# Dummy matmuls in the buffer of the step that follows, and a new order of steps, in a fused attention and MLP kernel

## The chip, the cores and the metric

One core of one Trainium2 chip. The metric is the device time of one execution in microseconds (us). Before the change it is 350.86 us, the median of 13 runs (348.72 to 353.51).

## What is computed

Attention over 8 batches, 8 heads, 576 positions and head size 64, with 16 extra "beacon" keys ahead of the 576 causal ones, and then a two-layer MLP over the 4608 tokens with an ELU between the layers:

```python
k_all = np.concatenate([beacon_k, k], axis=2)
v_all = np.concatenate([beacon_v, v], axis=2)
scores = scale * np.matmul(q, k_all.transpose(0, 1, 3, 2))
scores = np.where(causal, -1000000000.0, scores)
a = np.exp(scores - scores.max(-1, keepdims=True))
a /= a.sum(-1, keepdims=True) + 1e-09
attn = np.matmul(a, v_all)
...
h = x @ w_in                                  # x: 4608 x 512, w_in: 512 x 2048
g = np.where(h > 0.0, h, np.exp(np.minimum(h, 0.0)) - 1.0)
out = g @ w_out                               # w_out: 2048 x 512
```

## The kernel before, in words

**An order written out.** The kernel defines small steps (functions under `@step`), and a list of 1351 words at its end calls them one by one (L611 on). Each word is a step's name and its numbers, `S.2.6` for example. A manual schedule keeps the list's order on every engine: each engine runs its own instructions in the order of the list, and waits on semaphores where data or a buffer isn't ready. A word such as `ld.3.0.0:V.1.0.1` has a gate: the load is issued only after the step named behind the colon, which sets how early a transfer joins the DMA queues. The list, the gates and the strings of buffer numbers in `slots` come from a planner outside the kernel.

**The steps**, with the engine of each and the lines of before:
- Loads, all issued by GpSimd (POOL), with a cast on the way: `lq` (q and k of batches 0 and 1 to SBUF, L163), `ld` (q and k of later batches, DRAM to DRAM as bf16 in four quarters each, tile `qkd`, L174), `lv` and `lb` (v and beacon v, L191 and L184), `wi` and `wo` (the two weights, L202 and L206).
- q and k have to be transposed. For batches 0 and 1 TensorE does it (`T`, L252, with an identity matrix that step `id` makes), and `cp` copies the result from PSUM on ACT or DVE (its last letter, A or V, L271). From batch 2 on, `ct` issues two DMA transposes on the queue of SyncE (SP), from `qkd` into one of eight `qk` buffers (L266); it needs all eight `ld` of its batch. `cb` adds the beacon keys (L260). A `ct` has the numbers of batch and head pair.
- `S` computes scores of a batch into PSUM (L303), `x` takes their exponential on ACT (L340), `m` applies the causal mask on DVE (L356), `a` adds up partial sums on DVE (L458).
- `L`, `W` (batch 0), `Y`, `Z` (other batches) multiply by ones and by v on TensorE (L369, L474). `n`, `N` take the reciprocal of the sum as Ln and Exp on ACT, `M`, `V` scale the result into the MLP's input `xT` on DVE (L429, L438, L513).
- `F` is the first MLP product (L538), in two halves; `e` (ACT, L551), `r` and `g` (DVE, L556 and L563) are the ELU; `G` is the second product (L579) in eight words per output tile. `o` copies an output tile from PSUM to one of three `osb` buffers (L592), on ACT or DVE by its last letter, and `s` writes it out from SP (L601). The very last tile, `os`, is copied half by DVE and half by ACT into two `osb` buffers and written from two queues (L608, L609).

The MLP of a tile of 512 tokens starts when its batch's attention is done (the first 512 tokens are split in two tiles of 256), so attention of the following batches and the MLP of the earlier ones are interleaved in the list.

**PSUM** is used as four buffers of two banks, tags S0 to S3. Every step that opens a PSUM tile calls `pair`, which takes the next number from the string `slots["S"]`. A buffer is free again when its last reader is done.

**Dummies.** `warm` (L214) issues matmuls on a tile of zeros, in pairs over 64 rows each, to keep TensorE busy where the plan has a gap. Before, each dummy group opens a PSUM tile of its own in the buffer that its word names: `warm.3.512.S.1` is three pairs of 512 columns in S1. There are 16 such words, all in front of the 100th word of the list, with 80 matmuls in all.

Of the kernel before, what the change touches and what calls it, by code (L numbers as in the profile page):

```python
# [17 lines left out]
def kernel(  # L18
# [193 lines left out]

    @step
    def warm(n_, cols, tag, slot_):  # L214

        w = psum.tile([P, 2, 512], FP32, tag=f"{tag}{slot_}", bufs=1, name="w")
        for _ in range(n_):
            for i in range(2):
                nc.tensor.matmul(  # L219
                    out=w[:, i, 0:cols], lhsT=zero[D * i:D * (i + 1), 0:P], rhs=zero[D * i:D * (i + 1), 0:cols],  # L220
                    start=True, stop=True, skip_group_check=True)
# [25 lines left out]
    @step  # L247
    def T(b, p, i):
        dst = tps[b, p, i] = pair("tqk", BF16)[:, 0, :]
        for r in range(R):  # L250
            for h in range(2):
                nc.tensor.transpose(  # L252
                    out=dst[D * h:D * (h + 1), PR * r:PR * (r + 1)],
                    in_=st[b, i][:, 2 * p + h, r, :],
                    identity=identb[0:PR, 0:PR],
                )
# [65 lines left out]
    @step  # L322
    def S_(b, *k_):
        s = sc[(b,) + k_] = pair()
        for (p, c0, c1, o0) in part(b, *k_):
            score(b, p, s, c0, c1, o0)
# [57 lines left out]
    @step  # L384
    def L(b, g):

        if g == "A":
            t = pair("la")[:, 0, :]
            for i in range(2):
                quad(b, i, 0, CUT, t[:, CUT * i:CUT * (i + 1)], None, i == 0)  # L390
            lt[b, g] = t
        else:
            t = pair("lt")
            for i in range(2):
                quad(b, i, CUT, S, t[:, i, 0:S - CUT], None, True)
            lt[b, g] = t[:, :, 0:S - CUT]
# [13 lines left out]
    def W(b, g, *i):  # L410
        half = i[-1]
        k_ = (b, g) + i[:-1]
        if k_ not in ut:
            ut[k_] = pair("ua")
# [67 lines left out]
    def Y(b, g):  # L482

        t = pair("lt")
# [9 lines left out]
    def Z(b, g, half):  # L494
        if (b, g, "t") not in ut:
            ut[b, g, "t"] = pair("ut")
# [26 lines left out]
    def F(t, i, s_):  # L523
# [4 lines left out]
        if s_ == 0:  # L528
            hp[t, i] = pair("hps")
# [38 lines left out]
    def G(t, tp, s_, k_):  # L568
        if s_ == 0 and k_ == 0:
            ob[t, tp] = [pair("ops")]  # L570
# [43 lines left out]
    warm.19.512.S.0 lq.0.1.2.4 lq.0.0.0.2 lq.0.0.2.4 lq.0.1.0.2 lq.0.1.4.8 lq.0.0.4.8 lq.1.0.0.4 id  # L614
    bs lv.0.2 bt T.0.1.0 bk T.0.1.1 cp.0.1.0.A warm.3.512.S.1 cp.0.1.1.V cb.0.0 S.0.1.3 cb.0.1
    cb.0.2 T.0.0.1 x.0.1.3 cb.0.3 S.0.1.1 lq.1.1.0.4:cb.0.2 cb.1.0 cp.0.0.1.V T.0.0.0 x.0.1.1
    S.0.1.2 lb.0:cb.0.0 T.0.2.1 lv.0.1 cp.0.0.0.A cp.0.2.1.V warm.1.512.S.3 warm.1.128.S.3 x.0.1.2
    S.0.0.0 tri warm.2.512.S.2 warm.1.224.S.2 x.0.0.0 T.0.2.0 lv.0.0:cp.0.0.0.A S.0.1.0 cp.0.2.0.V
    T.0.3.0 x.0.1.0 warm.1.512.S.3 warm.1.96.S.3 wi.0.1 cp.0.3.0.V S.0.2.2 T.0.3.1 x.0.2.2
    wi.0.0:cp.0.1.1.V S.0.2.0 cp.0.3.1.V warm.2.512.S.1 warm.1.416.S.1 lv.0.4 x.0.2.0 S.0.3.2  # L620
    S.0.2.3 S.0.3.0 x.0.3.2 m.0.2.0 m.0.0.0 warm.1.512.S.0 warm.1.416.S.0 x.0.3.0 wi.1.0:m.0.2.0
    m.0.1.3 T.1.0.1 cb.1.1 S.0.3.3 x.0.2.3 cp.1.0.1.V lq.1.0.4.8:m.0.1.3 T.1.0.0 x.0.3.3 cp.1.0.0.V
    S.0.0.3 wi.1.1 warm.1.512.S.0 warm.1.384.S.0 m.0.3.2 x.0.0.3 lq.1.1.4.8:cb.0.1 S.1.2 m.0.1.0
    warm.3.512.S.1 warm.1.320.S.1 m.0.3.0 x.1.2.0 wi.2.0 L.0.A wi.3.0:cp.0.2.0.V W.0.A.1 n.0.A
    S.0.0.2 S.0.3.1 W.0.A.0 lv.0.3 x.0.3.1 S.1.0 M.0.A.1 x.0.0.2 wi.2.1 M.0.A.0 T.1.1.1 x.1.0.0
    F.0.0.0 cp.1.1.1.A S.1.1 T.1.1.0 x.1.1.0 F.0.0.1 cp.1.1.0.V wo.2:cp.1.1.1.A m.0.3.3 S.1.5
    m.0.2.2 S.0.0.1 T.1.3.0 x.0.0.1 cp.1.3.0.V e.0.0 S.0.2.1 m.0.0.2 F.0.1.0 m.0.0.3 x.0.2.1 r.0.0
    wo.1:m.0.0.3 F.0.1.1 m.0.2.3 x.1.5.1 wi.3.1:r.0.0 m.0.1.2 g.0.0 T.1.2.1 ld.2.1.144:m.0.1.2 e.0.1
    L.0.B cp.1.2.1.A r.0.1 T.1.2.0 n.0.B cb.1.2 S.1.3 cp.1.2.0.V ld.2.0.288:cb.1.2 g.0.1 T.1.3.1
    x.1.3.1 W.0.B.0.0 x.1.3.0 cb.1.3 cp.1.3.1.V S.1.4 ld.2.0.144:g.0.1 F.0.2.0 x.1.4.1 m.1.0.0  # L630
    W.0.B.0.1 S.1.6 M.0.B.0.0 W.0.B.1.0 x.1.6.2 m.1.3.1 cb.2.0 M.0.B.0.1 W.0.B.1.1 wo.0:M.0.B.0.0
    x.1.6.1 S.1.10 M.0.B.1.1 wo.3:M.0.B.0.1 F.0.2.1 x.1.10.3 M.0.B.1.0 F.1.1.0 ld.2.1.0:M.0.B.1.0
    e.0.2 S.1.9 F.1.1.1 r.0.2 x.1.9.2 m.1.4.1 F.1.0.0 x.1.9.3 g.0.2 ld.2.1.288:r.0.2 e.1.1 S.1.7
    F.1.0.1 m.1.6.1 x.1.7.2 cb.2.1 r.1.1 F.0.3.0 e.1.0 g.1.1 ld.2.0.0:r.1.1 F.1.2.0 r.1.0 S.1.11
    F.0.3.1 cb.2.2 m.1.5.1 x.1.11.3 lb.1:r.1.0 g.1.0 F.1.2.1 ld.2.1.432:m.1.5.1 e.0.3 m.1.10.3
    S.1.12 m.1.1.0 G.0.0.0.0 e.1.2 r.0.3 cb.2.3 G.0.0.0.1 g.0.3 x.1.12.3 lv.1.0:cb.2.3 G.0.0.0.2
    m.1.9.3 cb.3.0 m.1.3.0 m.1.11.3 G.0.0.0.3 ld.2.0.432:m.1.3.0 m.1.2.0 a.1.0.1 F.1.3.0 a.1.1.1
    S.1.8 r.1.2 F.1.3.1 lv.1.1:a.1.1.1 x.1.8.2 a.1.1.2 G.0.0.1.0 g.1.2 e.1.3 lv.1.3:a.1.1.2
    G.0.0.1.1 r.1.3 lv.1.2:g.1.2 G.1.0.0.0 a.1.1.3 g.1.3 lv.1.4:a.1.1.3 G.1.0.0.1 ct.2.0 cb.3.1
    a.1.0.2 G.1.0.0.2 m.1.8.2 m.1.9.2 G.0.0.1.2 a.1.0.3 m.1.12.3 lb.2:m.1.9.2 a.1.1.4 G.0.0.1.3  # L640
    a.1.0.4 lv.2.3:m.1.12.3 m.1.6.2 ct.2.1 o.0.0.V Y.1.0 Z.1.0.0 N.1.0 m.1.7.2 Z.1.0.1 cb.3.2
    a.1.3.1 ct.2.2 S.2.0 a.1.2.1 G.1.0.0.3 lv.2.2:a.1.3.1 x.2.0.0 V.1.0.2 a.1.3.2 S.2.2 a.1.2.2
    G.1.0.1.0 x.2.2.0 V.1.0.0 lv.2.0:a.1.2.2 S.2.1 a.1.3.3 G.1.0.1.1 ct.2.3 x.2.1.0 a.1.3.4 m.2.2.0
    lv.2.1:a.1.3.3 S.2.3 V.1.0.1 G.1.0.1.2 x.2.3.1 lv.2.4:m.2.2.0 S.2.5 x.2.3.0 m.2.3.1
    ld.3.0.0:V.1.0.1 S.2.4 a.1.2.3 x.2.5.1 G.1.0.1.3 m.2.3.0 a.1.2.4 m.2.0.0 ld.3.0.144:m.2.3.0
    S.2.6 x.2.4.1 m.2.5.1 Y.1.1 m.2.1.0 o.1.0.V ld.3.0.288:m.2.5.1 Z.1.1.1 N.1.1 Z.1.1.0 m.2.4.1
    ld.3.0.432:o.1.0.V x.2.6.1 S.2.8 V.1.1.1 x.2.6.2 V.1.1.0 x.2.8.2 S.2.7 a.2.0.1 F.2.0.0
    ld.3.1.0:V.1.1.0 x.2.7.2 m.2.6.1 V.1.1.2 S.2.10 a.2.0.2 F.2.0.1 ld.3.1.144:m.2.6.1 x.2.10.3
    a.2.1.1 a.2.0.3 F.2.2.0 a.2.1.2 e.2.0 m.2.8.2 a.2.1.3 S.2.11 F.2.2.1 x.2.11.3 r.2.0 F.2.3.0
# [124 lines left out]
```

## Time and profile before

| | before |
|---|---|
| median of 13 runs | 350.86 us |
| lowest, highest | 348.72, 353.51 us |
| the profiled execution | 350.86 us |
| its span (first to last instruction) | 349.1 us |
| TensorE (PE) busy | 331.3 us, 95% |
| DVE, ACT, POOL busy | 254.7, 206.8, 99.6 us |
| dummies on PE (L219) in the chain that ended last | 3% |
| end of the last matmul | 343.8 us |

The page of a profile shows, per engine, busy time and its share of the span, then the span in 40 slices with a digit for the busy tenths of each slice, then DMA queues, then the chain of work that ended last, then groups of instructions by source line with their mean length and the idle time ahead of them, and who ended it. PE is the matmul row; PEld is the loading of weights, which overlaps it; a dummy counts as busy. "X <- Y: total, times, longest" in the table of waits says how long X sat idle until Y was done.

### The profile page before, as it was taken

The page shows a single profiled execution, that of the slowest core. Times are in us where ns is not written, and L with a number is a line of the kernel's source. Part 1 is how long each engine was busy: PE and PEld are TensorE (multiplying, and loading weights), DVE is VectorE, ACT ScalarE, POOL GpSimd, SP SyncE. Part 2 cuts the span into 40 slices and gives each one's busy share as a digit, 9 for nine tenths or more (in the row PEclk, how much of TensorE's full clock was granted, in tenths as well). Part 3 has the DMA queues.
Part 4 walks back from the last instruction along what each step waited for, and adds up shares of the span by engine and source line. Part 5 has one row for each costly group of instructions (what it writes and reads, how often), then busy time and mean ns, then how long its engine had stood idle before and what let it go on. Part 6 is the DMA issues. An engine that isn't in the chain of part 4 may idle for free.

```text
span 349.1 us, 10876 instructions
## 1 busy us (share of the span) xinstructions
PE 331.3 (95%) x4716; PEld 186.6 (53%) x4716; DVE 254.7 (73%) x586; ACT 206.8 (59%) x247; POOL 99.6 (29%) x126
## 2 busy tenths in 40 slices
PE   8988999889999899999879999999999999999993
PEld 3556876455555455555435555555455555555551
DVE  1567799789988899799959997598964876685000
ACT  1799872697598795899658668744432343242111
POOL 7664446556181455164333001200000000000000
PEclk9999999999999999999989999999999999999998
DMA  8999999999999999999999834443000000300027
GB/s 130 173 157 201 168 159 103 158 125 89 141 132 201 135 165 94 103 148 92 126 163 98 182 62 30 32 132 124 0 2 2 0 2 0 122 3 0 2 88 274
DMA packets 137536, 35.97 MB, mean 103 GB/s; under 512 B 125712, under 2 KB 132880, under 8 KB 137488
## 3 DMA queue, kind: packets, MB, share of 16 engines
q0 software_dynamic: 102240, 18.49, 70.7%
q1 hardware_dynamic: 34528, 16.39, 23.1%
q8 instruction: 37, 0.61, 0.8%
q10 hardware_dynamic: 720, 0.39, 0.4%
q14 instruction: 11, 0.09, 0.1%
HBM read 37.22 MB, written 16.52 MB: 154 GB/s over the span
## 4 chain that ended last, share of the span: by engine, by line
PE 82%; DMA 6%; DVE 5%; ACT 3%; issue 1%; SPq 1%; DVEq 0%; ACTq 0%
PE hps L538 31%; PE ops L579 31%; PE sc L303 7%; PE ut L369 5%; DMA qk<-qkd 4%; PE w L219 3%; DVE gt L563 2%; ACT et L340 2%; DMA v<-in_v_dram 2%; DVE gt L556 1%; PE lt L369 1%; PE tqk L252 1%; DMA out_dram<-osb 1%; PE ua L369 1%; PE lt L474 1%
## 5 line engine op out<-in xcount | busy, mean ns | idle before, releaser
L538 PE MATMUL hps<-xT,w_in 64*128 64x512 f16 (+1 forms) x1280 | 139.1, 355 | 1.0 <-DVE xT L438 0.3
L579 PE MATMUL ops<-w_out,gt 64*128 64x512 f16 x1152 | 139.2, 378 | 0.0
L340 ACT ACTIVATE et<-sc 128x1024 f16<-128x1024 f32 (+4 forms) x128 | 105.6, 865 | 34.0 <-PE sc L303 32.6
L551 ACT ACTIVATE e<-hps 128x1024 f32<-128x1024 f32 x72 | 72.7, 1023 | 57.2 <-PE hps L538 57.2
L538 PEld LDWEIGHTS <-w_in 64*128 64x128 f16 x1280 | 68.4, 94 | 50.7 <-issue 2.2
L579 PEld LDWEIGHTS <-gt 64*128 64x128 f16 x1152 | 62.4, 94 | 53.6 <-issue 0.9
L563 DVE TENSOR_TENSOR gt<-hps,gt 128x1024 f16<-128x1024 f32 x72 | 87.4, 1221 | 3.2
L556 DVE TENSOR_SCALAR gt<-e 128x1024 f16<-128x1024 f32 x72 | 50.5, 702 | 21.8 <-ACT e L551 21.2
L191 POOL DMA_DIRECT2D v<-in_v_dram x40 | 34.1, 854 | 75.7 <-DVE xT L429 23.8
L356 DVE TENSOR_TENSOR et<-et,triu 128x256 f16<-128x256 f16 (+6 forms) x185 | 38.9, 254 | 10.9 <-ACT et L340 10.9
L303 PE MATMUL sc<-qk 64*128 64x80 bf16 (+20 forms) x528 | 40.2, 250 | 6.9 <-DMA qk<-qkd 4.7
L303 PEld LDWEIGHTS <-qk 64*128 64x128 bf16 x528 | 24.0, 95 | 25.0 <-DMA qk<-qkd 5.5
L458 DVE TENSOR_TENSOR ls<-ls,et 128x672 f16<-128x672 f16 (+2 forms) x84 | 29.0, 367 | 0.3
L174 POOL DMA_DIRECT2D qkd<-in_k_dram x24 | 21.6, 918 | 18.7 <-DVE et L356 5.1
L369 PEld LDWEIGHTS <-v 128*32 128x32 f16 x1248 | 20.7, 96 | 11.2 <-issue 3.4
L174 POOL DMA_DIRECT2D qkd<-in_q_dram x24 | 21.7, 923 | 16.0 <-DVE et L356 7.6
L592 ACT COPY osb<-ops 128x1024 f32<-128x1024 f32 x9 | 9.1, 1009 | 23.6 <-PE ops L579 19.8
L429 DVE TENSOR_TENSOR xT<-ut,rl 128x448 f16<-128x448 f32 (+6 forms) x56 | 20.0, 415 | 0.6 <-ACT rl L504 0.5
L369 PE MATMUL ut<-et,v 128*32 128x512 f16 (+4 forms) x560 | 19.1, 278 | 0.1
L608 DVE COPY osb<-ops 128x512 f32<-128x512 f32 x1 | 0.7, 691 | 24.6 <-PE ops L579 24.6
L503 ACT ACTIVATE rl<-lt 128x576 f32<-128x576 f32 x14 | 9.1, 653 | 14.4 <-PE lt L369 14.4
L458 DVE TENSOR_TENSOR ls<-et 128x928 f16<-128x928 f16 x28 | 17.4, 633 | 0.3 <-PE lt L474 0.2
(45 smaller groups left out, 127.1 us busy)
## 6 DMA issues: line engine op xcount, KB each, us to landing
out_dram<-osb SPq DMA_DIRECT2D x17, 512.0 KB, 4.0
qkd<-in_k_dram POOLq DMA_DIRECT2D x24, 144.0 KB, 4.7
qkd<-in_q_dram POOLq DMA_DIRECT2D x24, 144.0 KB, 4.8
v<-in_v_dram POOLq DMA_DIRECT2D x24, 128.0 KB, 5.5
w_in<-in_moe_w_in_dram POOLq DMA_DIRECT2D x8, 256.0 KB, 7.8
w_out<-in_moe_w_out_dram POOLq DMA_DIRECT2D x4, 512.0 KB, 7.8
v<-in_v_dram POOLq DMA_DIRECT2D x8, 112.0 KB, 4.1
stg<-in_k_dram POOLq DMA_DIRECT2D x3, 288.0 KB, 6.1
```

The costliest lines, as they stand in the source:

```text
L174: nc.gpsimd.dma_start(out=st[b, i][s0:s1], in_=(q, k)[i][b, :, s0:s1].rearrange("h s d -> s h d"))
L191: nc.gpsimd.dma_start(out=v_tile(b)[r0:r0 + n_, j, :, :], in_=v[b, :, ilo[j]:ilo[j] + n_, :].rearrange("h s d -> s h d"))
L303: nc.tensor.matmul(out=s[:, h, o0 + a - c0:o0 + e - c0], lhsT=t[D * h:D * (h + 1), 1, P * j:P * (j + 1)], rhs=t[D * h:D * (h + 1), 0, NB + ...
L340: nc.scalar.activation(out=ets[b, p][:, :, c0:c1], in_=s[:, :, o0:o0 + c1 - c0], func=AFT.Exp, bias=0.0, scale=SCALE)
L356: nc.vector.tensor_tensor(out=o, in0=o, in1=triu[0:kc[j], :, t0:t0 + e - a], op=ALU.mult)
L369: nc.tensor.matmul(out=t[32 * i:32 * (i + 1), a - qa:e - qa], lhsT=ones[0:kc[j], :] if half is None else v16[0:kc[j], j, h, half::2], rhs= ...
L458: nc.vector.tensor_tensor(out=lsum[b, p][0:kc[j], :, qj - q1:], in0=in0, in1=e_[0:kc[j], :, cj:cj + S - qj], op=ALU.add)
L538: both.append(nc.tensor.matmul(out=hp[t, i][:, out_, w * u:w * (u + 1)], lhsT=w_in16[rows, cc, P * fc:P * (fc + 1)], rhs=xt[k_][rows, cc, ...
L551: nc.scalar.activation(out=eb[t, i], in_=hp[t, i], func=AFT.Exp, bias=0.0, scale=1.0)
L556: nc.vector.tensor_scalar(out=rb[t, i], in0=eb[t, i], scalar1=1.0, scalar2=1.0, op0=ALU.min, op1=ALU.subtract)
L563: nc.vector.tensor_tensor(out=gt, in0=hp[t, i], in1=gt, op=ALU.max)
L579: both.append(nc.tensor.matmul(out=o_[out_][:, 0, :] if len(o_) == 2 else o_[0][:, out_, :], lhsT=gts[t, fc][rows, P * (2 * tp + out_):P * ...
```

## The change

The code gets two new helpers and one changed step. `warm` may now name the step that comes next instead of a buffer (`warm.6.496.own.L.0.A`): it opens that step's PSUM tile itself, through `pair`, so in the buffer that the step will use, writes the dummies there and leaves the tile in `made`. The step then takes it through `tile_of`, and overwrites it. For steps `S`, `F` and `G` the dummies are pairs of half rows in both banks, as before; for the others they are single matmuls over all 128 rows in the second bank.

The list of words and the buffer strings are new throughout, from the planner with a second case of late DMA landings beside the first. All steps other than dummies occur as often as before; of the 16 `cp`, four change from DVE to ACT and three from ACT to DVE, and of the output copies `o` one changes to DVE and three to ACT. Dummy words are now 11, with 58 matmuls.

```diff
     slots = {
         "et": (
-            "087625413807256148307521684037512680"),
+            "082476153804276513048725613408752614"),
         "S": (
-            "03210321032013201320123021302013202323201210321301303231010232012121021032031232"
...
+            "03213203120312013012301203210231021212002302130232032120233122302023023123103020"
...
-    @step
-    def warm(n_, cols, tag, slot_):
-
-        w = psum.tile([P, 2, 512], FP32, tag=f"{tag}{slot_}", bufs=1, name="w")
+    def fill(t, n_, cols, halves):
+
         for _ in range(n_):
-            for i in range(2):
+            if halves:
+                for i in range(2):
+                    nc.tensor.matmul(
+                        out=t[:, i, 0:cols], lhsT=zero[D * i:D * (i + 1), 0:P], rhs=zero[D * i:D * (i + 1), 0:cols],
+                        start=True, stop=True, skip_group_check=True)
+            else:
                 nc.tensor.matmul(
-                    out=w[:, i, 0:cols], lhsT=zero[D * i:D * (i + 1), 0:P], rhs=zero[D * i:D * (i + 1), 0:cols],
+                    out=t[:, 1, 0:cols], lhsT=zero[:, 0:P], rhs=zero[:, 0:cols],
                     start=True, stop=True, skip_group_check=True)
+
+    @step
+    def warm(n_, cols, slot_, *word_):
+
+        if slot_ != "own":
+            fill(psum.tile([P, 2, 512], FP32, tag=f"S{slot_}", bufs=1, name="w"), n_, cols, True)
+            return
+        f_, *k_ = word_
+        if f_ == "T":
+            t = pair("tqk", BF16)
+        else:
+            t = pair({"S": "sc", "F": "hps", "G": "ops"}.get(f_, "lt"))
+        made[word_] = t
+        fill(t[:, :, 0:1024].bitcast(FP32) if f_ == "T" else t, n_, cols, f_ in "SFG")
+
+    made = {}
+
+    def tile_of(f_, k_, *how):
+        return made.pop((f_,) + tuple(k_), None) or pair(*how)
...
     def S_(b, *k_):
-        s = sc[(b,) + k_] = pair()
+        s = sc[(b,) + k_] = tile_of("S", (b,) + k_)
...
-            t = pair("la")[:, 0, :]
+            t = tile_of("L", (b, g), "la")[:, 0, :]
...
```

`T`, `W`, `Y`, `Z`, `F` and `G` take their tiles through `tile_of` in the same way. The first words of the two lists:

```diff
-    warm.19.512.S.0 lq.0.1.2.4 lq.0.0.0.2 lq.0.0.2.4 lq.0.1.0.2 lq.0.1.4.8 lq.0.0.4.8 lq.1.0.0.4 id
-    bs lv.0.2 bt T.0.1.0 bk T.0.1.1 cp.0.1.0.A warm.3.512.S.1 cp.0.1.1.V cb.0.0 S.0.1.3 cb.0.1
...
+    warm.13.496.own.T.0.0.0 lq.0.0.0.2 lq.0.1.2.4 lq.0.0.2.4 lq.0.1.0.2 lq.0.1.4.8 lq.0.0.4.8 tri id
+    bs T.0.0.0 lq.1.1.0.4:bs T.0.1.0 T.0.1.1 lq.1.0.0.4 cp.0.1.0.V warm.3.448.own.S.0.1.3 cp.0.1.1.A
+    cp.0.0.0.A S.0.1.3 bt x.0.1.3 S.0.1.2 bk T.0.0.1 x.0.1.2 cb.0.0 warm.2.288.own.S.0.1.0 cb.0.1
+    cp.0.0.1.V S.0.1.0 T.0.2.1 x.0.1.0 m.0.1.2 S.0.1.1 cb.0.2 m.0.1.3 warm.5.432.own.T.0.2.0 cb.0.3
+    x.0.1.1 cp.0.2.1.V T.0.2.0 lq.1.0.4.8:cp.0.2.1.V S.0.0.0 cp.0.2.0.A T.0.3.1
+    warm.1.336.own.S.0.2.3 lv.0.2:cp.0.1.0.V x.0.0.0 cp.0.3.1.V S.0.2.3 S.0.2.2 x.0.2.2 T.0.3.0
+    lb.0:cp.0.3.1.V warm.5.416.own.S.0.3.0 cp.0.3.0.V x.0.2.3 lv.0.0:cb.0.3 S.0.3.0 m.0.2.3 T.1.0.0
+    lv.0.1:bk x.0.3.0 S.0.2.0 cp.1.0.0.V T.1.1.0 x.0.2.0 wi.0.1 S.0.0.2 cp.1.1.0.V T.1.0.1
+    cp.1.0.1.A S.0.3.1 m.0.3.0 warm.2.496.own.S.1.2 wi.0.0:cp.1.1.0.V m.0.0.0 x.0.0.2 S.1.2
+    warm.6.496.own.L.0.A m.0.2.0 wi.1.1 x.1.2.0 m.0.0.2 cb.1.0 wi.1.0:cp.0.3.0.V m.0.1.0 cb.1.1
+    x.0.3.1 lq.1.1.4.8 L.0.A W.0.A.0 n.0.A lv.0.4:m.0.0.0 S.0.3.3 W.0.A.1 wi.2.0:cb.0.2 x.0.3.3
+    S.0.3.2 M.0.A.1 S.0.0.3 lv.0.3:m.0.2.0 x.0.3.2 M.0.A.0 T.1.1.1 wi.2.1:m.0.3.0 x.0.0.3 F.0.0.0
...
```

On SP's queue the order of transposes and output writes, per batch, goes from `s.2.0 s.1.0 ct.4.0 ct.4.1 ct.4.2 s.2.1 ct.4.3` to `s.0.0 ct.4.0 ct.4.1 ct.4.2 ct.4.3 s.1.0 s.2.0`, from `ct.6.0 ct.6.1 ct.6.2 s.3.1 ct.6.3` to `ct.6.0 ct.6.2 ct.6.1 ct.6.3 s.2.1 s.3.1`, and from `ct.3.3 ct.3.0 ct.3.1 ct.3.2` to `ct.3.0 ct.3.1 ct.3.2 ct.3.3`. The last words are these:

```diff
-    G.9.1.0.1 G.9.0.1.2 G.8.0.1.0 G.8.0.1.1 G.9.1.0.2 G.9.0.1.3 G.9.1.0.3 o.9.0.A G.8.0.1.2 s.9.0
-    s.6.1 G.8.0.1.3 s.7.1 G.9.1.1.0 G.9.1.1.1 o.8.0.A G.9.1.1.2 G.9.1.1.3 s.8.0 os.9.1
+    G.8.1.0.3 G.9.1.0.2 G.9.1.0.3 G.8.1.1.0 G.8.1.1.1 G.8.1.1.2 G.9.0.1.1 G.9.1.1.0 G.8.1.1.3
+    G.9.0.1.2 o.8.1.A G.9.1.1.1 G.9.0.1.3 G.9.1.1.2 o.9.0.A G.9.1.1.3 s.9.0 os.9.1 s.8.1
```

## The prediction

> **What bounds the kernel now.** I read the page's slices first, then the stages, then TensorE's waits, then the timeline at each long wait and at the end. In the slices each digit is a tenth of 8.7 us.
>
> ```profile
> PE   8988999889999899999879999999999999999993
> ...
> DVE  1567799789988899799959997598964876685000
> ...
> PEclk9999999999999999999989999999999999999998
> DMA  8999999999999999999999834443000000300027
> ```
>
> TensorE is full from about 185 us to 344 us, so a change can only win in the first 185 us, or after 344 us. The stages (stage, length, then busy time of PE, PEld, DVE, ACT, POOL, granted clock, DMA share, GB/s) say where PE isn't full:
>
> ```profile
> 8.00:26.00 18.00, 15.98 (x328) 9.76 (x330) 10.63 (x32) 14.63 (x20) 11.60 (x17) 1.00 1.39 166
> ...
> 165.00:185.00 20.00, 16.88 (x241) 8.87 (x238) 15.66 (x40) 13.55 (x17) 7.38 (x9) 0.91 1.72 137
> ...
> 205.00:344.00 139.00, 138.82 (x1569) 74.30 (x1565) 87.10 (x138) 56.07 (x62) 4.22 (x5) 1.00 0.17 43
> ```
>
> Busy PE is not useful PE, since the dummies count. So I made a ledger: every PE step of the list at its own pitch in the trace (an F or G step 0.863 us, T 0.376, S 0.2 to 0.3, Y 0.56, Z 0.59). F and G give 248.3 us, all the rest 59.8: 308.1 us of useful work, and the same in both kernels, because the same steps are only reordered. PE ends at 343.8. The lost 35.7 us are 1.3 before its first instruction, 13.6 in dummies (from a dummy's start to the next step's; the first group alone is 6.2) and 20.7 in waits and pitch above these values. The longest waits are for DMAs:
>
> ```profile
> PE sc L303 <- DMA qk<-qkd: 4.7, 2, 3.1
> ...
> PE lt L369 <- DMA v<-in_v_dram: 1.6, 2, 1.3
> ```
>
> The timeline (start, length, what, idle time before it) puts them at three places, a v load at 62 us and transposed q and k at 121 us and 176 us:
>
> ```profile
> 62.63 0.24 PE L369 MATMUL lt<-et,v 128*32 128x64 f16 x8 [1.32 <-DMA v<-in_v_dram]
> ```
>
> ```profile
> 121.57 0.28 PE L303 MATMUL sc<-qk 64*128 64x256 bf16 x2 [1.63 <-DMA qk<-qkd]
> ```
>
> ```profile
> 176.51 0.39 PE L303 MATMUL sc<-qk 64*128 64x256 bf16 x2 [3.05 <-DMA qk<-qkd]
> 176.70 1.91 PE L579 MATMUL ops<-w_out,gt 64*128 64x512 f16 x8
> ```
>
> Against the ledger they cost 1.92, 2.04 and 4.50 us. The third is more than its wait: the eight matmuls after it occupy PE for 1.71 us until the next step instead of 0.86, with the slices' 8 in PEclk at that place.
>
> **What the Trainium skill says.** "TensorE: Matmul & The Clock Gate", part 1 on the HAM clock gate: an idle window of about 3.4 us drops PE to half clock. The trace agrees (3.05 us idle, then a doubled pitch). The same page, part 2, step by step: matmuls stay in program order, so one late operand holds all behind it; at 176 us ready G steps stood behind S.6.6. "DMA: Bandwidth & Descriptors", "Issuing engines are not separate DMA queues": SP's and POOL's transfers interleave on the same 16 engines. The trace agrees: four v loads landed 2.7, 2.5 and 0.5 us apart (57.3, 60.1, 62.6, 63.1) while transposes ran, and 1.0 to 1.2 us apart for larger qkd loads when none did (99.9 to 104.0).
>
> **The change part by part.** Sums are against the profiled execution: 350.86 us, span 349.1, and the median of the 13 runs is 350.86 too.
>
> *Dummies, first matmuls.* The first group goes from 38 half-row matmuls in pairs (6.17 us) to 13 full ones. Nine pairs at 0.43 us ran before the clock rose at 5.07; 13 at that pitch end before 6.9. T.0.0.0 then needs the identity: POOL has issued six loads by 5.37, then tri (0.82) and id (0.70), so 6.9. Before, bt began at 7.58 and S.0.1.3 at 9.51; now T.0.0.0 at 7.0, three T steps, a copy on ACT (0.64) from 8.2: S.0.1.3 at 8.95. From there I followed the longest of PE, ACT and DVE: S.1.2 at 18.5 (was 21.05), the masks of all four pairs done at 20.6, so L.0.A at 20.65 (was 22.41). From L.0.A to F.0.0.0 the trace has 3.49 us (Ln and Exp 1.26, two scalings 1.3): F.0.0.0 at 24.1 instead of 25.90, with 0.16 us more useful work done. Gain: about **2.0 us**. A dummy now takes the buffer of its own step, so it can't start until that buffer is free; the six in front of L.0.A (1.24 us) get theirs at about 18.5 and end by 20, hidden by DVE's masks. If that cover is gone, they cost their full length; all dummies after the first group are 4.96 us, the upper bound. At best this part gains 4.
>
> *Loads of the start.* Three loads for batch 1 (1.6 us of service each) go ahead of v and w_in, and lq.1.0.4.8 waits for cp.0.2.1.V (about 13.0), with lv.0.2 to wi.0.0 queued behind it on POOL. Summing the landing pitches (288 KB 1.6, w_in 1.25, w_out 2.55, qkd 0.95, v 0.55 to 0.65): wi.0.0 lands at about 23 (was 20.1), just in time for F.0.0.0; the last load of batch 2 at 52 to 53 (was 55.8), as more is issued early and the queue stays full. The transposes of ct.2.0 land 7.1 us later (56.0 to 63.1 before): 59 to 60. lv.1.4 has now 2.6 us of PE work between it and the load before it, and lands about 58 to 59.5. PE reaches Y.1.0 at 58.8 (41.5 useful plus 17.3 lost) and S.2.0 at about 60. So most of the 1.92 us goes: **1.3 us**, between 0 and 1.9.
>
> *Transposes, batches 3 to 6.* I count useful PE work between the SP step and its first reader. ct.3.0 to S.3.0: 4.0 before, 6.2 after. ct.4.2 to S.4.6: 5.8, now 6.4. ct.6.2 to S.6.6: 4.8, now 11.0. The trace's need, issue to landing of both halves, is 4.0 to 4.5 us with nothing beside it (ct.6.1, ct.5.1), 6.8 for ct.4.2, 8.4 for ct.6.2. In both slow cases other transfers ran: lv.4.1 to lv.4.3 and the output write s.2.1, lv.6.2 to lv.6.4 and s.3.1. After the change lv.4.0 to lv.4.3 stand ahead of ct.4.0, and no output write stands inside a batch's four transposes: s.0.0 follows ct.3.3, s.1.0 and s.2.0 follow ct.4.3, s.2.1 and s.3.1 follow ct.6.3. Gain at 121 us **1.7** of 2.04 (0 to 2.04), at 176 us **4.4** of 4.5 (2.5 to 4.5), with the half clock, which needs the idle. New risk: ct.3.0 has v loads just before it; I take **0.4** lost, 0 to 1.5. Next late would be DVE: from 74 to 173 us it is busy 89.95 of 99 us, where PE has 92.4 of useful work; the cover for the 1.7 is thin.
>
> *End.* The last output tile uses two of three osb buffers. The lines from before:
>
> ```profile
> 337.86 1.01 ACT L592 COPY osb<-ops 128x1024 f32<-128x1024 f32 x1 [6.80 <-PE ops L579]
> ...
> 343.90 0.69 DVE L608 COPY osb<-ops 128x512 f32<-128x512 f32 x1 [24.59 <-PE ops L579]
> ...
> 345.15 0.59 ACT L608 COPY osb<-ops 128x512 f32<-128x512 f32 x1 [1.49 <-DMA out_dram<-osb]
> 345.76 0.38 ACTq L609 DMA_DIRECT2D out_dram<-osb  x1
> ```
>
> The ACT half waited for s.7.1's landing at 345.07; its own write landed at 347.83, 4.0 us after PE's end, and the span closed 1.3 later. After, s.8.1 is the last word, so 8.1's buffer is still held, and the ACT half must take 9.0's. With PE's end as zero: o.9.0 starts at -1.7 (two G steps remain), s.9.0 issues at -0.6 and lands at about +2.2 (2.8 us, as s.8.0 and s.8.1), copy 0.59, issue, landing 2.07 later: +5.0. s.8.1, behind the DVE half on SP, issues at +1.2 and lands at +4.0 to +4.9. So the end is **1.0 us later** (0.5 to 1.8).
>
> *Copies* that change between ACT and DVE: one more on ACT (0.64), one output copy fewer on DVE: nothing, covered by idle ACT (34 us before et alone).
>
> Sum: 350.86 - 2.0 - 1.3 - 1.7 - 4.4 + 0.4 + 1.0 = **342.9 us**.
>
> **Rivals.** *The stalls move.* All 13 runs lie between 348.7 and 353.5; none shows the 8 us that three absent stalls would give, so the lateness belongs to the list. A new list may bring its own late landings, or DVE, full to 93% from 74 to 173 us once 1.7 us are gone, may hold PE. Then only the start and half of 176 us remain: 350.86 - 2.0 - 2.2 + 1.0 = 347.7. For it: 1.2 us lost in small pieces between 131 and 166 us with no named stall. Against: the longer leads above.
>
> *Slower: the load chain behind lq.1.0.4.8.* POOL issues in order, so if cp.0.2.1.V or what feeds it is late, v, w_in, w_out and batch 2 are late by as much. With the three batch-1 loads not hidden (4.8 us) and the queue empty before lq.1.0.4.8 (the eighth load would land at 14.5, the ninth at 17.5, 1.6 of that service: 1.4) the last load of batch 2 lands at 55.8 + 6.2 = 62.0, ct.2.0 at 69.1, S.2.0 then instead of at 64.6 with 0.6 less work done: 5.1 lost, half clock for one window 1.7 more, and the gains of the first 65 us (3.3) gone: 342.9 + 3.3 + 5.1 + 1.7 = 353.0. It decides once that load lands after about 60. For it: lead ct.2.0 to S.2.0 falls from 4.3 to 3.7. Against: the chain summed above has 6 us of slack to that point.
>
> *No effect:* the waits vary by themselves and the leads are eaten by later issues: 350.9.
>
> **How the numbers follow.** Forecast 0.55 (339 to 346), stalls move 0.24, slower 0.12, no effect 0.09. The range 339 to 350 leaves out the slower case, half of no effect and a few in a hundred below. About 0.5% (1.75 us) can be told from no change: faster 0.76 (forecast, nearly all of the moved stalls), same 0.12, slower 0.12.
>
> **What would show it.** F.0.0.0 near 24 us and S.2.0 near 60; no PE wait for qk above 0.5 us at batches 4 and 6; PEclk without the 8 in mid-span; from PE's last matmul to the span's end 6.3 us instead of 5.3. Wrong would be: a PE wait on v or qk over 2 us anywhere, dummies standing behind a buffer's release, or DVE without gaps where PE idles.

## The result, and the profile after

The changed kernel takes 343.96 us, the median of 11 runs (343.27 to 345.60), against 350.19 us for 48 runs of the kernel before (347.68 to 353.51): a ratio of 0.983, with a 95% interval of 0.981 to 0.986. This ratio, and those of the experiments, leave out the runs that took over 1.5% more than the fastest of their kernel, so they aren't quite the quotients of the medians. The change is worth 6.2 us; the forecast was 342.9. The profiled execution of the changed kernel has a span of 342.7 us, against 349.1.

The slices of the changed kernel's page:

```profile
PE   7979999989999999999999999999999999999992
...
DVE  1667599799999999788999987798876456783000
...
PEclk9999999999999999999999999999999999999999
DMA  8999999999999999999899554421000013003104
```

PE is now nearly full from about 25 us on, apart from an 8 around 72 us; the lower digits that it had around 60, 120 and 175 us and the 8 in PEclk in mid-span are gone. The stages (same columns as in the prediction) say the same in numbers:

```profile
8.00:26.00 18.00, 15.72 (x333) 10.05 (x335) 11.45 (x37) 15.30 (x21) 10.84 (x16) 1.00 1.22 146
...
165.00:185.00 20.00, 19.92 (x361) 11.80 (x358) 19.21 (x51) 15.77 (x20) 9.60 (x11) 1.00 1.36 139
```

From 165 to 185 us PE is busy 19.92 of 20 us at full clock, where it was 16.88 at 0.91. The first stage is no fuller than before (15.72 us against 15.98). In the table of PE's waits no line for `qk` is left, and none for `v`; what leads it now lies in the first 75 us:

```profile
PE hps L560 <- DMA w_in<-in_moe_w_in_dram: 1.4, 1, 1.4
...
PE hps L560 <- DVE xT L451: 1.2, 1, 1.2
...
PE tqk L274 <- DMA stg<-in_q_dram: 0.8, 1, 0.8
```

The timeline of the changed kernel shows those places, then batch 6, then the end:

```profile
25.47 1.05 PE L560 MATMUL hps<-xT,w_in 64*128 64x256 f16 x16 [1.38 <-DMA w_in<-in_moe_w_in_dram]
...
72.07 1.04 PE L560 MATMUL hps<-xT,w_in 64*128 64x512 f16 x8 [1.24 <-DVE xT L451]
...
171.13 0.40 PE L325 MATMUL sc<-qk 64*128 64x176 bf16 x6
171.35 1.04 PE L560 MATMUL hps<-xT,w_in 64*128 64x512 f16 x8
...
336.58 0.69 DVE L630 COPY osb<-ops 128x512 f32<-128x512 f32 x1 [24.62 <-PE ops L601]
...
338.69 0.59 ACT L630 COPY osb<-ops 128x512 f32<-128x512 f32 x1 [2.89 <-DMA out_dram<-osb]
```

F.0.0.0 (first line) waits for w_in. S.6.6 at 171.13 has no idle time in brackets, and the eight matmuls behind it take their normal length. At the end the ACT half waits 2.89 us for the landing of s.9.0, and the span closes 6.2 us after PE's last matmul (336.48), against 5.3 before.

With the ledger of the prediction (lag is the start of a PE step less the useful work done before it), stretch by stretch, the profiled executions against each other:

| Stretch | lag gained before, us | lag gained after, us | gain | forecast |
|---|---|---|---|---|
| to F.0.0.0 | 16.29 | 15.70 | 0.6 | 2.0 |
| F.0.0.0 to S.2.0 (62 us) | 5.08 | 3.48 | 1.6 | 1.3 |
| S.2.0 to Y.3.0 | 3.52 | 4.39 | -0.9 | -0.4 |
| Y.3.0 to F.3.5.0 (batch 4) | 2.27 | 0.23 | 2.0 | 1.7 |
| F.3.5.0 to F.4.6.0 | 1.55 | 1.86 | -0.3 | 0 |
| F.4.6.0 to Y.5.1 (batch 6) | 5.22 | 0.85 | 4.4 | 4.4 |
| PE's end to the span's end | 5.28 | 6.22 | -0.9 | -1.0 |

The seven gains add up to 6.5 us, the span is 6.4 us shorter, and the 0.1 us between them lies in the last 150 us.

### The profile page after: what moved, and what is told of

Its sections match the earlier page's. It is cut to its first block, busy times and chain, and to the rows that moved or that the text cites. A ratio compares the mean times of both kernels' runs of the same rounds, so it can differ in the third digit from the quotient of the medians.

```text
span 342.7 us, 10834 instructions
## 1 busy us (share of the span) xinstructions
PE 329.1 (96%) x4694; PEld 187.0 (55%) x4694; DVE 252.1 (74%) x583; ACT 209.1 (61%) x250; POOL 98.5 (29%) x126
## 4 chain that ended last, share of the span: by engine, by line
PE 85%; DVE 6%; DMA 4%; ACT 2%; issue 1%; POOL 0%; DVEq 0%; ACTq 0%; POOLq 0%
PE ops L601 36%; PE hps L560 32%; PE sc L325 6%; PE ut L391 4%; DVE gt L585 3%; DMA w_in<-in_moe_w_in_dram 2%; PE lt L391 2%; DMA stg<-in_q_dram 2%; PE lt L496 1%; DVE gt L578 1%; PE tqk L274 1%; DVE qk L293 1%; DMA out_dram<-osb 1%; PE ua L391 1%; ACT e L573 1%
## 5 line engine op out<-in xcount | busy, mean ns | idle before, releaser
L362 ACT ACTIVATE et<-sc 128x1024 f16<-128x1024 f32 (+4 forms) x128 | 104.5, 866 | 21.2 <-PE sc L325 19.7
L378 DVE TENSOR_TENSOR et<-et,triu 128x256 f16<-128x256 f16 (+6 forms) x185 | 38.0, 253 | 8.4 <-ACT et L362 8.4
L325 PE MATMUL sc<-qk 64*128 64x64 bf16 (+16 forms) x528 | 39.1, 247 | 0.2
L325 PEld LDWEIGHTS <-qk 64*128 64x128 bf16 x528 | 23.1, 94 | 16.5 <-ACT qk L293 1.4
L614 ACT COPY osb<-ops 128x1024 f32<-128x1024 f32 x11 | 11.1, 1011 | 25.1 <-PE ops L601 25.1
L480 DVE TENSOR_TENSOR ls<-et 128x928 f16<-128x928 f16 x28 | 17.5, 634 | 0.3
```

Of the source, the lines that this page charges most:

```text
L325: nc.tensor.matmul(out=s[:, h, o0 + a - c0:o0 + e - c0], lhsT=t[D * h:D * (h + 1), 1, P * j:P * (j + 1)], rhs=t[D * h:D * (h + 1), 0, NB + ...
L362: nc.scalar.activation(out=ets[b, p][:, :, c0:c1], in_=s[:, :, o0:o0 + c1 - c0], func=AFT.Exp, bias=0.0, scale=SCALE)
L378: nc.vector.tensor_tensor(out=o, in0=o, in1=triu[0:kc[j], :, t0:t0 + e - a], op=ALU.mult)
L480: nc.vector.tensor_tensor(out=lsum[b, p][0:kc[j], :, qj - q1:], in0=in0, in1=e_[0:kc[j], :, cj:cj + S - qj], op=ALU.add)
```

## The experiments

My theory: the transposes of batches 4 and 6 were late because they were issued too few PE steps ahead of their readers and other transfers ran beside them, and the new order mends both; where the dummies write matters little; the tail is dearer. Rivals: the dummies' own tiles give the gain; or output writes inside the transposes alone made the stalls; or the stalls come from the leads alone. Twelve experiments in three groups (1 to 4, 5 to 8, 9 to 12), each beside runs of the kernel before, whose medians in the groups were 349.52, 350.18 and 349.94 us. Ratios are to the runs of the same group.

**1. The dummies taken out.** The list without its ten later dummy words:

```diff
- ... cp.0.1.0.V warm.3.448.own.S.0.1.3 cp.0.1.1.A ...
+ ... cp.0.1.0.V cp.0.1.1.A ...
- ... m.0.3.0 warm.2.496.own.S.1.2 ... S.1.2 warm.6.496.own.L.0.A ...
+ ... m.0.3.0 ... S.1.2 ...
```

> The changed kernel (343.96 us) without its ten later groups of dummies, 4.96 us of PE in all; the first group stays. Dummies are no part of the computation. Theory (they stand where PE would wait anyway): within 0.5%, 342.5 to 345.5, and PE's waits grow by about what the dummies took. Rival (a dummy now waits for its step's own buffer, so it runs late and stands on the path): down to 339, up to 4.96 us faster. Second rival (they keep the clock up): 345.5 to 349, with an 8 or less in PEclk in the first 60 us.

Measured: 346.5 us (342.22 to 347.92), ratio 0.987 [0.981, 0.994]. The time alone can't be told from that of the changed kernel (0.983 [0.981, 0.986]), but the sign that the second rival named is there. The page of this kernel has a 6 in PEclk in the first 60 us:

```profile
PEclk9969999899999999999999999999999999999998
```

The windows (stage, length, PE, PEld, DVE, ACT, POOL, clock, DMA, GB/s) of the changed kernel from 8 to 17.5 us:

```profile
8.00:17.50 9.50, 8.94 (x179) 5.80 (x181) 5.80 (x16) 7.82 (x11) 3.92 (x6) 1.00 1.06 148
```

and of this one from 8 to 24.3 us:

```profile
8.00:17.50 9.50, 6.96 (x160) 4.89 (x156) 7.09 (x19) 9.04 (x13) 4.76 (x7) 1.00 1.24 158
17.60:24.30 6.70, 5.97 (x113) 3.86 (x115) 3.28 (x16) 6.19 (x9) 6.25 (x9) 0.50 1.41 169
```

Without the dummies PE is busy for 6.96 us of the first stretch instead of 8.94, and then the clock stands at 0.50 from 17.5 to 24.4 us. That isn't one trace alone: the mean granted clock of the six runs of this kernel is 0.967 to 0.985, that of 18 runs of the changed kernel 0.991 to 0.999 (and of the six of kernel 3, in the same group as this one, 0.993 to 0.999). So the dummies hold the clock up.

F.0.0.0 came earlier all the same, at lag 13.94 instead of 15.70 (14.82 in another trace of the changed kernel, experiment 5), so dummies stand on the path there as well. At S.2.0 all of it was gone (lag 19.24 against 19.18), because ct.2.0 landed at 61.82, no earlier than elsewhere in the changed list (59.46 in experiment 5). The timeline of this kernel there, and its window:

```profile
61.86 0.60 PE L325 MATMUL sc<-qk 64*128 64x512 bf16 x2 [2.17 <-DMA qk<-qkd]
62.26 1.91 PE L601 MATMUL ops<-w_out,gt 64*128 64x512 f16 x8
```

```profile
62.00:63.00 1.00, 1.00 (x6) 0.30 (x4) 0.00 (x0) 0.50 (x1) 0.14 (x1) 0.50 1.60 164
```

The time saved early became a wait of 2.17 us, and behind it the clock was at 0.50 again: eight G matmuls take 1.91 us. At F.2.0.0 this kernel lags by 22.66, the changed kernel by 21.22.

**2. The dummies' part of the change alone.** The kernel before, order and slots unchanged, with the new `fill`, `tile_of` and `warm`:

```diff
- ... cp.0.1.0.A warm.3.512.S.1 cp.0.1.1.V ...
+ ... cp.0.1.0.A warm.3.512.own.S.0.1.3 cp.0.1.1.V ...
```

> The kernel before, its order and slots unchanged, but every group of dummies after the first writes into the tile of the step that follows it. It is the first half of the change alone. Theory (the gain is in the order, not in where the dummies write): 349 to 352, no difference. Rival (the dummies' own tiles give the gain): 344 to 347. Second rival (they wait for the step's buffer and then delay the step itself): 352 to 355.

Measured: 349.9 us (22 runs), ratio 1.001 [0.999, 1.004]. No difference, as the theory has it, but not because nothing happens. In the trace of the kernel before, the line of the dummies after the first group is this:

```profile
L219 PE MATMUL w<-zero x42: 199/373/387, 8.5 to 22.2; 64*128 64x512 bf16 x28, 64*128 64x416 bf16 x4, 64*128 64x128 bf16 x2, 64*128 64x224 bf16 x2
its engine sat idle before it (us, times) until:
  issue: 2.5, 7
```

PE sat idle 2.5 us ahead of those dummies, and the profile names nobody for it. With the step's own tile the idle time is gone: from the first dummy of each of the eight groups to the step behind them it was 7.32 us in all, and is 4.83 here. (Three of the eight, ahead of `T` and `L` steps, are now also single matmuls over all rows; the five with the same matmuls as before went from 4.36 to 2.81 us.) S.1.2 comes at 19.11 instead of 21.05. But the timeline of this kernel at batch 4 shows where that went:

```profile
113.21 0.39 PE L327 MATMUL sc<-qk 64*128 64x64 bf16 x4 [1.20 <-DMA qk<-qkd]
...
118.94 0.34 PE L327 MATMUL sc<-qk 64*128 64x384 bf16 x2 [2.48 <-DMA qk<-qkd]
...
122.70 0.28 PE L327 MATMUL sc<-qk 64*128 64x256 bf16 x2 [1.58 <-DMA qk<-qkd]
```

The last load of batch 4 was issued 2.7 us earlier than before (100.67 against 103.40) and landed at the same time (110.27 against 110.34). PE came sooner and waited longer: 6.1 us of lag between Y.3.0 and F.3.5.0 instead of 2.27.

**3. The tail undone.** The changed kernel, one word moved:

```diff
- G.9.0.1.2 o.8.1.A G.9.1.1.1 ... s.9.0 os.9.1 s.8.1
+ G.9.0.1.2 o.8.1.A s.8.1 G.9.1.1.1 ... s.9.0 os.9.1
```

> The changed kernel with the output write s.8.1 moved from the last place of the list to directly behind its copy o.8.1.A, so the third osb buffer is free before the end. Theory (the tail grew by 0.94 us because the last ACT copy waits for s.9.0's landing): 342.6 to 343.2, 0.8 to 1.4 us faster, and from PE's end to the span's end 5.0 to 5.4 us instead of 6.2. Rival (the tail is set by the last landing on SP's queue in any case): 343.7 to 344.3, no difference.

Measured: 343.65 us (342.15 to 345.94), ratio 0.983 [0.979, 0.988]. The trace is clear, the time isn't. The timeline of this kernel at its end:

```profile
335.67 0.69 DVE L630 COPY osb<-ops 128x512 f32<-128x512 f32 x1 [24.62 <-PE ops L601]
336.37 0.59 ACT L630 COPY osb<-ops 128x512 f32<-128x512 f32 x1 [1.49 <-DMA out_dram<-osb]
```

The ACT half starts 0.8 us after PE's end (335.56) instead of 2.2, and the span ends 4.8 us after it.

**4. Only the output writes moved, in the old order.** The kernel before, with two words moved:

```diff
- ... s.2.1 cb.4.3 x.4.3.1 a.3.2.2 ct.4.3 ...      ... s.3.1 r.4.7 Z.5.0.0 ct.6.3 ...
+ ... cb.4.3 x.4.3.1 a.3.2.2 ct.4.3 s.2.1 ...      ... r.4.7 Z.5.0.0 ct.6.3 s.3.1 ...
```

> The kernel before with only two output writes moved out of the transposes: s.2.1 behind ct.4.3 and s.3.1 behind ct.6.3. Theory of the writes (a write beside the transposes makes them land late): the waits for qk at 121 and 176 us shrink from 1.63 and 3.05 us to under 0.5, and the time is 344 to 346. Theory of the leads (the transposes were issued too few PE steps ahead of their reader, and the v loads beside them are enough to make them late): both waits stay above 1 us, and the time is 349 to 351.

Measured: 349.64 us (22 runs), ratio 1.000 [0.997, 1.002]. Moving the writes alone gives nothing. Its table of PE's waits has nearly the same sum as before:

```profile
PE sc L303 <- DMA qk<-qkd: 4.6, 3, 3.0
```

In this trace the wait at batch 4 is 3.0 us, though no write is near ct.4.2 (issued at 116.25, landed at 124.41), and the one at batch 6 is 1.02 us: the lag over batch 4 grew from 2.3 to 4.4 us and that over batch 6 shrank from 5.2 to 1.9. Kernel 2, with the write inside, has 6.1 and 2.0 there, so traces of the old list divide the loss between the two places differently, and an effect of the write can't be seen in it.

**5. The changed kernel once more**, without an edit.

> The changed kernel once more, without an edit, beside the runs of this group, since single traces differ by 1 to 2 us in the first 20 us. Expected: 343 to 345 us, 6.2 us from PE's end to the span's end, no wait for qk above 0.5 us at batches 4 and 6, and F.0.0.0 between 24.5 and 26.

Measured: 344.39 us (343.71 to 346.56), ratio 0.987 [0.982, 0.991]; no wait for `qk` at all, the tail again 6.2 us, F.0.0.0 at 24.59 and lag 14.82. So in the start two traces of one kernel differ by 0.9 us, and the gain there is 0.6 to 1.5 us against the trace of before.

**6. Batch 6 of the changed kernel with the old load and the writes inside.**

```diff
- ... m.5.5.1 ld.6.1.432:m.5.3.1 cb.7.0 ...   ct.6.0 ... ct.6.2 ... ct.6.1 ... ct.6.3 ... s.2.1 ... s.3.1
+ ... V.4.1.0 ld.6.1.432:V.4.1.0 ...          ct.6.0 ct.6.1 ... ct.6.2 s.2.1 s.3.1 ... ct.6.3
```

> The changed kernel with batch 6 put back to what it was: its last load (ld.6.1.432) waits for V.4.1.0 again, the transposes stand in the order 0, 1, 2, 3, and the output writes s.2.1 and s.3.1 stand behind ct.6.2, inside them. Theory (the load's lead and the writes made the stall at 176 us): the wait for qk at S.6.6 comes back at 1 to 3 us, with half clock behind it, and the time is 345.5 to 348.5. Rival (the gain at batch 6 comes from elsewhere in the new list): within 0.5% of the changed kernel, 342.3 to 345.5.

Measured: 345.15 us (343.78 to 347.55), ratio 0.988 [0.983, 0.993]. The stall did not come back, so the first theory fails here: ct.6.2, issued at 164.03, landed at 169.80, and PE reached S.6.6 at 170.64. One v load, lv.6.2, was issued beside it at 166.15.

**7. The changed kernel with only the writes inside.**

```diff
- ... e.4.3 ct.6.2 F.4.5.0 ... N.5.0 s.2.1 Z.5.0.1 s.3.1 G.4.0.0.0 ...
+ ... e.4.3 ct.6.2 s.2.1 s.3.1 F.4.5.0 ... N.5.0 Z.5.0.1 G.4.0.0.0 ...
```

> The changed kernel with only the output writes s.2.1 and s.3.1 moved back among batch 6's transposes, behind ct.6.2. Theory of the leads (with the load 19 us ahead of its reader a write inside does no harm): no wait at S.6.6 over 0.5 us, 343 to 345.5, no difference from the changed kernel. Theory of the writes (a write beside the transposes is what makes them late): a wait of 1 us or more at S.6.6 or its neighbours, 345 to 348.

Measured: 344.25 us (343.17 to 345.13), ratio 0.985 [0.980, 0.989]. No difference and no wait for `qk`. (In this trace the clock is at 0.50 from 24.65 to 28.07 us, though its list is the changed kernel's up to the transposes of batch 6: the start varies from trace to trace.)

**8. Two w_in loads early.**

```diff
- ... lq.1.0.0.4 cp.0.1.0.V ... wi.0.1 ... wi.0.0:cp.1.1.0.V ...
+ ... lq.1.0.0.4 wi.0.1 wi.0.0 cp.0.1.0.V ...
```

> The changed kernel with two w_in loads, wi.0.1 and wi.0.0, moved directly behind lq.1.0.0.4, ahead of the waiting lq.1.0.4.8, so that the queue has work from 15 to 17.8 us. Theory (F.0.0.0 waits 1.38 us for wi.0.0, which stands behind that wait, and the gap of 1.4 us in the queue shifts all later loads): no wait for w_in, F.0.0.0 at 24.1 to 24.6, last load of batch 2 about 54, S.2.0 0.5 to 1.3 us earlier, 342.6 to 343.4. Rival (xT on DVE is ready no sooner, so another wait takes its place): F.0.0.0 at 25 or later, no difference. Slower rival (v and the loads of batch 1 land 2.5 us later and hold L.0.A or T.1.3.0): 344.5 to 346.5.

Measured: 344.49 us (343.84 to 345.22), ratio 0.986 [0.982, 0.990]. The rival holds: F.0.0.0 at 25.20. Its table of PE's waits shows three others in place of the one taken away:

```profile
PE ua L391 <- DMA v<-in_v_dram: 0.7, 1, 0.7
PE ua L391 <- ACT rl L426: 0.7, 1, 0.7
PE hps L560 <- DMA stg<-in_k_dram: 0.7, 1, 0.7
```

What went ahead in the queue pushed v and batch 1's k back, as the slower rival said, though not so far that the time shows it.

**9. Batch 6 all back.** As kernel 6, and the v loads earlier as well:

```diff
- ... lv.6.2:g.4.5 ... lv.6.3:V.5.0.0 ... lv.6.4:V.5.0.1 ...
+ ... r.4.3 lv.6.2:r.4.3 ... r.4.4 lv.6.3:r.4.4 g.4.4 lv.6.4:g.4.4 ...
```

> The changed kernel with batch 6 put back as in the run before it (last load late, transposes in the order 0, 1, 2, 3, two output writes inside) and now also the v loads lv.6.2 to lv.6.4 issued among the transposes, as the kernel before had them. Theory of the v loads (they share the engines with ct.6.2, which then takes 7 to 8.4 us instead of 5.8): ct.6.2 lands at 171 to 172.5, S.6.6 waits 0.5 to 2 us for qk, 345 to 347. Rival (the stall needs the whole old list): no wait over 0.3 us, 344 to 345.5.

Measured: 344.24 us (343.61 to 346.07), ratio 0.983 [0.979, 0.988]. The rival holds: no wait. It is close, though: ct.6.2 took 6.7 us (164.07 to 170.77), and PE came to S.6.6 at 170.73. It isn't quite the old case: the v loads were issued at 160.7, 163.0 and 164.3, two of them ahead of ct.6.2, and in the kernel before at 168.0 to 171.1, together with it.

**10. Only the v loads moved, in the old order.** The kernel before, seven words moved:

```diff
- lv.4.1:cb.4.2 ... lv.4.2:V.3.0.1 ... lv.4.3:a.3.3.1 ... ct.4.3 lv.4.4:cb.4.3 ...
+ ct.4.3 ... r.3.2 lv.4.1:V.3.0.0 lv.4.2:V.3.0.0 lv.4.3:V.3.0.0 lv.4.4:V.3.0.0 ...
- ct.6.2 lv.6.2:m.5.7.2 ... lv.6.3:r.4.6 ... ct.6.3 lv.6.4:g.4.6 ...
+ ct.6.2 ... ct.6.3 ... V.5.0.0 lv.6.2:V.5.0.0 lv.6.3:V.5.0.0 lv.6.4:V.5.0.0 ...
```

> The kernel before with only seven v loads moved: lv.4.1 to lv.4.4 wait for V.3.0.0 and lv.6.2 to lv.6.4 for V.5.0.0, so that none is issued among the transposes of batches 4 and 6. Theory of the v loads: ct.4.2 and ct.6.2 land within 5.5 us of their issue instead of 6.8 and 8.4, the waits at 121 and 176 us shrink below 1 us, 345 to 347.5. Theory of the leads (the transposes come too few PE steps ahead of their readers, whatever runs beside them): the waits stay above 1.5 us, 349 to 351.

Measured: 345.32 us (344.74 to 346.87), ratio 0.986 [0.981, 0.991]. Seven loads moved in the old list give 4.6 of the 6 us (3.1 to 6.6 by the interval). Its table of PE's waits:

```profile
PE sc L303 <- DMA qk<-qkd: 1.5, 1, 1.5
PE lt L369 <- DMA v<-in_v_dram: 1.4, 2, 1.1
```

The wait at 176 us is gone (lag from F.4.6.0 to Y.5.1: 0.90 instead of 5.22). The one at batch 4 has only moved from ct.4.2's reader to ct.4.1's: 1.99 us of lag from S.4.0 to F.3.5.0 as against 2.07. So the expectation held in the time and at batch 6; at batch 4 ct.4.2 took 5.9 us, and a wait of 1.5 us stayed. The table of DMA issues shows what changed at batch 6 (transfer, issuing queue, count, KB each, median us from issue to landing), over the issues of ct.6.2 and ct.6.3. First the kernel before, 168 to 174 us:

```profile
v<-in_v_dram POOLq DMA_DIRECT2D x2, 128.0 KB, 6.7
...
qk<-qkd SPq DMA_TRANSPOSE x4, 7.6
```

and the kernel of this experiment, 166.4 to 173.2 us:

```profile
out_dram<-osb SPq DMA_DIRECT2D x1, 512.0 KB, 5.1
qkd<-in_q_dram POOLq DMA_DIRECT2D x1, 144.0 KB, 4.4
qk<-qkd SPq DMA_TRANSPOSE x4, 5.0
```

The four transposes land in 5.0 us instead of 7.6, with the output write and a load still beside them.

**11. Both, in the old order**: kernel 10 with the two writes moved as in kernel 4.

> The kernel before with both edits: the seven v loads as in the run beside it, and the output writes s.2.1 and s.3.1 behind the transposes. Nothing else then runs beside ct.4.2 and ct.6.2. Theory (other transfers, not the lead alone, make them late): 344 to 346.5, waits for qk at batches 4 and 6 below 0.5 us each. Theory of the leads: 348.5 to 351.

Measured: 346.37 us (345.48 to 348.24), ratio 0.989 [0.985, 0.994]. No better than the v loads alone, and at batch 4 1.7 us of lag remain (Y.3.0 to F.3.5.0). Its waits for `qk` are four, two at batch 3 (0.42 and 0.61 us) and two at batch 4 (0.76 and 0.22):

```profile
PE sc L303 <- DMA qk<-qkd: 2.0, 4, 0.8
```

**12. The tail undone, again**: the kernel of 3, for a second time.

> The changed kernel with s.8.1 directly behind o.8.1.A once more, for a second time and trace. Theory (six traces of the changed list and its variants end 6.2 to 6.3 us after PE, the one with this edit 4.8): a tail of 4.7 to 5.0 us again, and 342.5 to 343.5. Rival (the first trace was chance): a tail of 6.2, 344 to 344.5.

Measured: 342.76 us (342.32 to 346.11), ratio 0.980 [0.975, 0.986], with a tail of 5.2 us. The two groups give 0.983 and 0.980, where the changed kernel has 0.983 and 0.987: about 1 us in favour, inside the intervals. The tail of 4.8 and 5.2 us against 6.2 is shown by the traces; that this version is the fastest is likely, and not shown by the times.

## Why the prediction was right, step by step

*The sum.* The forecast was 8.0 us of gain, and 6.2 were measured. That 342.9 lies only 1.1 us from 343.96 is in part luck: the base of the sum, 350.86 from 13 runs, was 0.7 us above the 350.19 of 48.

*Batch 6 (4.4 forecast, 4.4 in the trace)* is right in size. Here too there is luck, since forecast and measurement go by the same trace of the old list. In the traces of kernels 2 and 4 batch 6 costs only 2.0 and 1.9 us, and batch 4 6.1 and 4.4. The two places together are a firmer figure: 7.5, 8.1 and 6.2 us in the three traces of the old order with its v loads in place, 1.1 in the changed kernel, so 5.1 to 7.0 gained where 6.1 was forecast.

In its reasons the prediction named two kinds of transfers beside the transposes, and only one can be seen to count. Set side by side, what ct.6.2 took from issue to its second landing, and how much time PE left it until S.6.6:

| kernel | v loads issued with ct.6.2 or up to 4 us later | write inside | took | time left |
|---|---|---|---|---|
| before | 3 | yes | 8.4 | 5.1 |
| 2: before, dummies' tiles | 3 | yes | 7.1 | 5.8 |
| 4: before, writes moved | 3 | no | about 7.2 | 5.9 |
| 10: before, v loads moved | 0 | yes | at most 6.2 | 6.2 |
| changed | 1 | no | 5.0 | 13.1 |
| 7: changed, writes inside | 1 | yes | 4.5 | 12.6 |
| 6: changed, late load, writes inside | 1 | yes | 5.8 | 6.6 |
| 9: the same, v loads ahead | 1, and 2 just ahead | yes | 6.7 | 6.7 |

(The value of kernel 4 is from the end of PE's wait, since one landing is missing in its trace; that of 10 is a bound, since nobody waited.) Three v loads go with 2 to 3 us more landing time than one or none; a write, issued 2.6 us or more after the first of the pair, with none that can be told. ct.5.1 shows the same the other way round: the changed order puts two v loads beside it, and it took 6.7 to 8.3 us in the nine traces of that order, 4.5 to 6.1 in the five of the old order with none beside it. The v loads are not all, though. In kernels 10 and 11 ct.4.1 took 7.5 and 6.6 us with no v load issued beside it.

The changed kernel mends batch 6 twice: transposes that take 3 us less, and 8 us more time for them. Either is enough, so taking the time back (kernels 6 and 9) brings no stall, and the old list with the v loads alone moved shows that they were the cause there: 0.9 us is lost at batch 6 in the traces of kernels 10 and 11, 1.9 to 5.2 in the three with the v loads in place. (Four loads of batch 4 were moved together with the three of batch 6, so the 4.6 us of kernel 10 belong to both places.)

*Batch 4 (1.7 forecast, 2.0)* has no shown cause. Against the trace of before, kernels 10 and 11 keep 1.7 to 2.1 us of 2.3; against those of kernels 2 and 4, with 6.1 and 4.4 us lost there, the v loads count at this place too (ct.4.2 took 6.8, 8.2 and 8.2 us with them, 5.9 and 5.1 without). For what remains the new order has two things that kernels 10 and 11 haven't. Its last load is earlier: ld.4.1.432 was issued at 100.75 and landed at 107.28, against 103.40 and 110.34, and ct.4.1 waits behind it on SP. And the output writes s.2.0 and s.1.0, which the old order issues together with that load (at 103.41 and 103.93), stand behind ct.4.3. An early issue alone doesn't do it: kernel 2 issued the load at 100.67, with both writes beside it, and it landed at 110.27. No run moved this load or these two writes alone, so longer lead and absent writes are both argued, not shown.

*Loads of the start, at 62 us (1.3, measured 1.6).* Right: no wait for v or `qk` is left there (S.2.0 at 61.80, and 60.65 in the second trace, where 60 was forecast). The last load of batch 2 landed at 55.45 instead of 52 to 53, which left the slower rival 4.5 us short of its point.

*ct.3.0's new risk (0.4 lost, measured 0.9).* Right in sign, wrong in place: nobody waits for ct.3.0. F.2.0.0 waits 1.24 us for `xT`, that is for DVE, which was named as what would be late next.

*The start (2.0 forecast, 0.6 and 1.5 in two traces)* is the term that was mis-sized. Up to L.0.A the marks held within 0.8 us (S.0.1.3 at 9.69 and 8.97 for 8.95; S.1.2 at 19.24 and 18.51 for 18.5; L.0.A at 20.94 and 20.21 for 20.65). The failed step is "from L.0.A to F.0.0.0 the trace has 3.49 us", with wi.0.0 landing at about 23 "just in time": it landed at 25.42 and 24.33, and F.0.0.0 came 4.53 and 4.38 us after L.0.A. Kernel 8 shows that it wasn't this load's place alone: with the load early, F.0.0.0 still stood at 25.20, behind other waits, two of them for transfers. What bounds this stretch as a whole stays open.

*Dummies.* That the tile of the step costs nothing was too simple. It saves 2.5 us of idle PE in the old order (kernel 2), and some of the later dummies stand on the path (kernel 1: 0.9 to 1.8 us by F.0.0.0). Neither gain reaches the end: a wait for `qk` further on takes it back, and in kernel 1 the half clock as well. That the dummies keep the clock up, which kernel 1 shows, stands nowhere in the working.

*End (1.0 later, measured 0.9)*: right, by the wait that was named, and kernels 3 and 12 take it away.

*Copies.* The working counts one output copy fewer on DVE; it is two (three go to ACT, one comes to DVE). No wait of PE in the changed kernel is for such a copy, so the term stays nothing.

*Rivals.* "The stalls move" was refuted in its main point: there is no wait for `qk` in any of the eight traces of the changed list with its dummies. What it was right about is the direction between the terms: in the old order, time gained in the first 60 us (kernel 2) did turn into longer stalls at 120 us. The sum was additive only because the same change took those stalls away.

*The clock.* The Trainium skill, "TensorE: Matmul & The Clock Gate", part 1, says that activity is watched in a free-running window of about 3.4 us. The traces agree, on the halving and on the window: in the clock records of all 14 the stretches between two changes of the clock are whole multiples of 3.41 us (3.41 and 6.83 at half clock; 10.24, 37.55 or 170.67 at full clock). So no length of idle time is a threshold by itself; what seems to count is how much of it falls into one such stretch. In the stretch ahead of the drop at 176 us PE was busy for 0.32 of the time, in that ahead of the drop at 62 us of kernel 1, with its wait of 2.17 us, for 0.36. The wait of 2.48 us in kernel 2 lay across the border of two stretches, the emptier one with PE busy for 0.51, and the clock stayed. That isn't the whole rule either: in kernel 1 the clock fell at 17.5 us after a stretch with 0.72, in kernel 7 at 24.65 us after one with 0.54, both where PE ran short matmuls and transposes.

## What to carry to other kernels

Before a late transfer is issued earlier, look at what is issued in the same microseconds: moving other loads, whose readers come over 20 us later, out of its way gave 4.6 us here with seven words. Compare, for each transfer that an engine waits for, the time from issue to landing with the time that its reader leaves it, and write both down; at batch 6 a remedy on either side was enough. Gains ahead of a place that DMA sets don't count until that place is mended. Take more than one trace before a loss is put down to one place: here three traces of one order divided the same loss in three ways.

## What was unexpected of the hardware

- A dummy group in a PSUM tile of its own costs PE more than its matmuls: 7.32 us for eight groups, against 4.83 us in the tile of the step that follows, with 2.5 us of idle time that the profile puts down to no releaser (4.36 against 2.81 us for the five groups whose matmuls are the same).
- Ten small groups of dummies, 45 matmuls, hold the clock: without them the mean granted clock of a run was 0.967 to 0.985, with them 0.991 to 0.999.
- The same pair of transposes, ct.6.2, took 7.1 to 8.4 us from issue to landing with three v loads of 128 and 80 KB issued in the same 4 us, and 4.5 to 6.5 us with one (6.7 with two more just ahead), whether or not 512 KB output writes were issued from 2.6 us on.
- The start of one list varies: F.0.0.0 of the changed list stood between 24.59 and 25.47 us in its traces here with an unedited start, which is as much as the changes of the start were worth.
